# An allowance in the planner behind the comparisons of the later routing phases

## The chip, the cores and the metric

The kernel runs on one core of one Trainium2 chip. The metric is the device time of one execution in microseconds. A program is compiled once and run several times; the median of the runs is what counts.

## What is computed

Three layers follow one another: causal attention with decay (4 batches, 8 heads, 576 positions, head size 64), a dense layer with a squared ReLU (512 to 2048 to 512 on 2304 tokens), and a layer of eight experts (512 to 1024 to 512). The change is in the third. Every token goes to one expert, and each expert takes at most 288. The reference goes through all pairs of token and expert from the highest logit down:

```python
logits = x @ w_gate                       # 2304 x 8
order = np.argsort(-logits.flatten())
for idx in order:
    tok, e = int(idx) // E, int(idx) % E
    if assigned[tok] >= 0 or counts[e] >= cap:   # cap = 288
        continue
    assigned[tok] = e
    counts[e] += 1
...
for e in range(E):
    h = np.maximum(x[assigned == e] @ w1[e], 0.0)
    out[assigned == e] = h @ w2[e]
```

## The kernel before, in words

**Routing in phases.** The kernel does not sort. In each of eight phases (`phase(m)`, m from 0 to 7) it finds the expert that is the next to be full, the threshold at which that happens, and the tokens that it gets. Logits lie in a tile L of 128 partitions, 18 columns and 8 experts. A phase takes each token's best remaining expert (L1005 to L1018) and then finds the threshold in three rounds, digit by digit of the logit's bits (`RND`). In a round VectorE compares a digit with a row of numbers in three groups of six columns: OH (one-hot, L1053) and G (greater or equal, L1056). TensorE multiplies OH by G over 18 columns and so gets a histogram (L1067). VectorE copies two columns of it (h0, L390, a helper); TensorE sums over experts (L1072); VectorE forms rs, counts (L1074, L1078) and PB (L1081); TensorE sums again (T8, L1082), and the result gives the digit (th, L1083). After the third round come the small operations of the tail: ef, gx, mE, tie, ASG and the two masks M (L1105 to L1114), the expert's number ei (L1116), a prefix sum and a column sum by TensorE (L1122, L1124), and the positions (L1129 to L1145). A last comparison, OR (L1149, in the same buffer as OH), and TensorE's list matmul over 18 columns (L1163) put the token numbers in order; `lo` and `idx` (L1167, L1169) are copied from it. Phase 7 has no histogram: it gives what is left to the last expert, so it has only the tail and a list. Each phase needs the marks (ASG) and the remaining places (r, L1182) of the one before.

**Experts.** `expert(m)` gathers 288 rows through idx (three indirect DMAs of GpSimd, L1195), loads the weights of expert ei (SyncE reads the number from SBUF and issues eight loads, L1214 or L1228), transposes the rows (L1259), multiplies up (L1279) and down (L1308), transposes back (L1324) and scatters (L1331, GpSimd). Experts 0 to 4 multiply in plain float32. For experts 5 to 7 each weight is split into a rounded part (ScalarE, L386) and a remainder (GpSimd, 128x512 subtractions of L1234), and three products are added (L1283 to L1285, L1311 to L1313). Buffers that matter here: OH and G have one buffer each in all phases; idx has three, so idx of phase m waits until expert m - 3 has been scattered; raw weights have four.

**The order.** All work is given to a planner, `Sched`, as operations with the engines that can do them, a fixed duration for each, and the buffers read and written. It runs a list schedule of its own in planned time: an engine that is free takes, among the operations that are ready, the one with the smallest priority number. Phase m has 20 + m, expert m has 30 + m (28.5 + m for its gather), so a phase's operation goes ahead of any expert's as soon as it is ready. The order that comes out is written into the program engine by engine, and on the chip each engine keeps it: an engine that reaches an operation whose input is late stands still. When an operation ends in the plan, those that depend on it become ready after a latency by pair of engines, to which the operation can add an allowance of its own, `lag`:

```python
rt = now + LAT.get(t.eng, {}).get(e, 100.0) + t.lag
```

The allowance is in planned time only; nothing waits for it on the chip. The kernel before uses it in the weights of the dense layer and nowhere in the phases.

Of the kernel before, what the change touches and what calls it, by code (L numbers as in the profile page):

```python
# [14 lines left out]
OP = mybir.AluOpType  # L15
# [312 lines left out]
def dve2(n):  # L328
    return 70 + 0.52 * n
# [42 lines left out]
class K:  # L372
# [589 lines left out]
    def phase(self, m):  # L962
        s, lc, pp = self.s, self.lc, self.pp
        L, ASG, w8, i0, i1 = self.L, lc["ASG"], lc["w8"], lc["i0"], lc["i1"]
        last = m == E - 1
        ra, rows = 1 << RA, 8 << RA

        def T(shape, dt, tag, n=1):
            return s.buf(pp, shape, dt, "ph_" + tag, n)

        def v(fn, r, w, n=18, ap=0):
            s.op({"dve": 63.0 + 1.04 * n + (60 if ap else 0)}, fn, r=r, w=w)

        def small(tag="sm"):

            if m == 0 and tag in ("H", "pl"):
                return s.buf(self.ps, [128, 512], F, tag + "0", 0, also=[("pt", 0)] if tag == "H" else [("sc", 0), ("sc", 1)])
            return s.buf(self.ps, None, F, tag, 0, also=[("rt", 0)] if tag == "H" else [("rt", 1 + j) for j in range(NSM)])

        def pairs(a, n):  # L980
            return a.rearrange("p (b t) -> p b t", t=2)[:, :, None, :].to_broadcast([128, a.shape[1] // 2, n, 2])

        mE = T([128, 1], F, "mE")
        M = T([128, 2, 18], BF, "M")
        if last:
            v(lambda e: e.tensor_copy(mE.t, lc["SE"].t), [lc["SE"]], [mE], 1)
            fr = T([128, 18], F, "fr") if m else None
            v(lambda e: e.tensor_scalar(fr.t, ASG.t, 0.0, None, op0=OP.is_equal), [ASG], [fr])
            v(lambda e: e.scalar_tensor_tensor(M[:, 0, :], ASG.t, mE[:, 0:1], fr.t, op0=OP.is_equal, op1=OP.add), [ASG, fr, mE], [(M, 0)], ap=1)
            v(lambda e: e.tensor_copy(M[:, 1, :], lc["zz"][:, 0:18]), [lc["zz"]], [(M, 1)])  # L990
        else:
# [30 lines left out]
            for rd, (ba, bb_) in enumerate(RND):  # L1022
# [4 lines left out]
                q = T([128, 18], BF, "q")  # L1027
                bb = T([128, 18], BF, "bb")
# [17 lines left out]
                OH = T([128, 9, 128, 2], BF, "OH")  # L1046
                G = T([128, 9, 128, 2], BF, "G")
                hist = small("H")
                groups = [(0, 6, 0), (6, 12, 0), (12, 18, 1)] if m == 0 and rd == 0 else [(0, 6, None), (6, 12, None), (12, 18, None)]
                for g, (t0, t1, pi) in enumerate(groups):  # L1050
                    sl = slice(t0 // 2, t1 // 2)
                    nt = t1 - t0
                    s.op({"dve": dve2(nt * rows)}, lambda e, sl=sl, OH=OH, q=q, t0=t0, t1=t1, nt=nt: e.tensor_tensor(  # L1053
                        OH[:, sl, :rows], i1.t[:, None, :rows].to_broadcast([128, nt // 2, rows, 2]), pairs(q[:, t0:t1], rows), op=OP.is_equal),
                        r=[i1, (q, pi)], w=[(OH, g)])
                    s.op({"dve": dve2(nt * W)}, lambda e, sl=sl, G=G, bb=bb, W=W, t0=t0, t1=t1, nt=nt: e.tensor_tensor(  # L1056
                        G[:, sl, :W], pairs(bb[:, t0:t1], W), i0.t[:, None, :W].to_broadcast([128, nt // 2, W, 2]), op=OP.is_ge),
                        r=[i0, (bb, pi)], w=[(G, g)])

                    if m:  # L1060
                        if t1 < 18:
                            continue
                        t0 = 0

                    def hm(e, OH=OH, G=G, hist=hist, W=W, t0=t0, t1=t1):
                        for t in range(t0, t1):
                            e.matmul(hist[:rows, :W], OH[:, t // 2, :rows, t % 2], G[:, t // 2, :W, t % 2], start=(t == 0), stop=(t == 17))  # L1067
                    s.op({"pe": (t1 - t0) * HM}, hm, r=[(OH, g), (G, g)] if m == 0 else [OH, G], w=[hist])
# [75 lines left out]
        rb = T([128, 18], BF, "rb")  # L1144
        v(lambda e: e.scalar_tensor_tensor(rb.t, gm[:, :, 1], -96.0, rr.t, op0=OP.mult, op1=OP.add), [rr, (gm, 1)], [rb])  # L1145
        OR = T([128, 9, 128, 2], BF, "OH")
        for g in range(2):
            t0, t1 = (0, 8) if g == 0 else (8, 18)
            s.op({"dve": dve2(96 * (t1 - t0))}, lambda e, t0=t0, t1=t1: e.tensor_tensor(  # L1149
                OR[:, t0 // 2:t1 // 2, :96], i1.t[:, None, :96].to_broadcast([128, (t1 - t0) // 2, 96, 2]), pairs(rb[:, t0:t1], 96), op=OP.is_equal), r=[i1, rb], w=[(OR, g)])  # L1150
            if g == 0:
                gi = T([128, 18, 3, 2], BF, "gi")
                v(lambda e: e.tensor_tensor(gi.t, gm.t[:, :, :, None].to_broadcast([128, 18, 3, 2]), lc["ids"].t[:, :, None, :].to_broadcast([128, 18, 3, 2]), op=OP.mult), [gm, lc["ids"]], [gi], 108)
                pl = small("pl" if m == 0 else "sm")

            if m:
                if g == 0:
                    continue
                t0 = 0

            def lm(e, t0=t0, t1=t1):
                for t in range(t0, t1):
                    e.matmul(pl[:96, 0:6], OR[:, t // 2, :96, t % 2], gi[:, t].rearrange("p g d -> p (g d)"), start=(t == 0), stop=(t == 17))  # L1163
            s.op({"pe": (t1 - t0) * LM}, lm, r=[(OR, g) if m == 0 else OR, gi], w=[pl])
# [278 lines left out]
```

## Time and profile before

| | |
|---|---|
| median of 3 runs | 970.78 us (966.82 to 972.22) |
| the profiled execution | 967.55 us |
| its span, first to last instruction | 965.8 us |
| mean granted TensorE clock | 0.982 of full |
| TensorE busy | 913.3 us, 95% |
| VectorE, ScalarE, GpSimd busy | 658.8, 393.4, 352.2 us |

The profile is of one execution. A timeline row gives the start in us from the span's start, the length in us, the engine (PE is TensorE, DVE is VectorE, ACT is ScalarE, POOL is GpSimd, SPq the queue of DMAs that SyncE issues), the line, the operation, the tiles out<-in and the count of instructions merged into the row. What stands in brackets is the idle time of that engine before it and the work that ended it. The output of a matmul is named by its PSUM bank: `ov` is the bank of the phases. A float32 matmul has two records.

### The profile page before, as it was taken

How to read it: one execution, taken by the hardware profiler on the slowest of the kernel's cores; microseconds unless marked ns; L12 is line 12 of the kernel's file. 1: busy time of each engine (PE TensorE's matmuls, PEld its weight loads, DVE VectorE, ACT ScalarE, POOL GpSimd, SP SyncE). 2: the span in 40 equal slices, each digit the busy share in tenths (PEclk: the TensorE clock that was granted, in tenths of full speed). 3: DMA queues.
4: the chain of work that ended last, by engine and by line, in shares of the span. 5: the costliest groups of instructions: out<-in, count | busy, mean ns of one | idle time of the engine just before them, and what ended most of it. 6: DMA issues, size and time to landing. Idle time of an engine off the chain costs nothing. (4 is left out here: it accounts for less than half of the span.)

```text
span 965.8 us, 17449 instructions
## 1 busy us (share of the span) xinstructions
PE 913.3 (95%) x6087; PEld 737.0 (76%) x6087; DVE 658.8 (68%) x2078; ACT 393.4 (41%) x1075; POOL 352.2 (36%) x467
## 2 busy tenths in 40 slices
PE   6999898999999999999999999995999999999995
PEld 3555564767778989898989899774777777789995
DVE  5999999987436999999954322676777787422231
ACT  4777576656654344444434366000001122235310
POOL 2455565555234353535231100002003032657911
PEclk9999899999999999999999999995999999999998
DMA  5769686553314010101000000038535451434400
GB/s 201 239 216 277 212 252 218 173 163 113 109 42 158 22 44 1 45 1 44 1 23 1 23 1 1 12 110 275 165 124 182 175 159 39 142 116 158 133 26 26
DMA packets 48617, 106.72 MB, mean 111 GB/s; under 512 B 10280, under 2 KB 18632, under 8 KB 48400
## 3 DMA queue, kind: packets, MB, share of 16 engines
q1 hardware_dynamic: 45456, 96.16, 30.3%
q0 software_dynamic: 3072, 9.44, 3.3%
q8 instruction: 48, 0.79, 0.3%
q14 instruction: 41, 0.34, 0.1%
HBM read 91.25 MB, written 14.33 MB: 109 GB/s over the span
## 5 line engine op out<-in xcount | busy, mean ns | idle before, releaser
L694 PE MATMUL u<-xh,z 128*128 128x256 f32 x512 | 148.9, 291 | 0.4 <-ACT r L699 0.3
L696 PE MATMUL u<-xl,z 128*128 128x256 f32 x512 | 144.8, 283 | 0.0
L695 PE MATMUL u<-xh,z 128*128 128x256 f32 x512 | 144.8, 283 | 0.0
L711 POOL TENSOR_TENSOR hl<-r,hh 128x256 fp32r<-128x256 f32 x96 | 88.7, 926 | 132.3 <-ACT hh L386 116.9
L699 ACT ACTIVATE r<-u 128x256 f32<-128x256 f32 x144 | 54.7, 380 | 155.5 <-PE u L696 125.4
L863 DVE CUSTOM_DVE_ANT_0 gjk<-wof,wgb 128x512 bf16<-128x512 f32 x128 | 109.0, 852 | 1.4
L694 PEld LDWEIGHTS u<-xh,z 128*128 128x128 f32 x512 | 97.2, 190 | 13.2 <-issue 3.4
L695 PEld LDWEIGHTS u<-xh,z 128*128 128x128 f32 x512 | 97.3, 190 | 7.7
L696 PEld LDWEIGHTS u<-xl,z 128*128 128x128 f32 x512 | 97.2, 190 | 0.0
L720 PE MATMUL acc<-z,hl 128*128 128x512 f32 x224 | 88.3, 394 | 2.9 <-POOL hl L711 2.6
L718 PE MATMUL acc<-z,hh 128*128 128x512 f32 x224 | 89.6, 400 | 0.5 <-ACT hh L386 0.5
L1308 PE MATMUL acc<-ehh,z 128*128 128x288 f32 x320 | 89.0, 413 | 0.0
L719 PE MATMUL acc<-z,hh 128*128 128x512 f32 x224 | 88.9, 397 | 0.0
L1279 PE MATMUL u<-exh,z 128*128 128x288 f32 x304 | 86.8, 423 | 0.0
L1234 POOL TENSOR_TENSOR z<-wr,z 128x512 fp32r<-128x512 f32 x48 | 59.8, 1280 | 43.6 <-ACT z L386 43.5
L526 ACT ACTIVATE p<-p,st 128x448 f32<-128x448 f32 (+4 forms) x110 | 61.1, 556 | 31.2 <-DVE st L519 28.8
L514 POOL TENSOR_TENSOR row<-maskb,row 128x128 f32<-128x128 bf16 (+1 forms) x90 | 44.3, 497 | 74.6 <-DVE st L519 57.6
L1308 PEld LDWEIGHTS acc<-ehh,z 128*128 128x128 f32 x320 | 56.9, 190 | 14.0 <-issue 0.7
L1279 PEld LDWEIGHTS u<-exh,z 128*128 128x128 f32 x304 | 55.8, 195 | 14.5 <-ACT exh L386 0.3
L1195 POOL DMA_INDIRECT xg<-x2d,ph_idx x24 | 25.3, 1055 | 100.3 <-DVE ph_fr L1011 52.3
L1331 POOL DMA_INDIRECT out_dram<-yo,ph_idx x24 | 24.3, 1011 | 100.3 <-DVE ph_P L1097 32.3
L700 ACT ACTIVATE r<-r 128x256 f32<-128x256 f32 x138 | 57.7, 418 | 4.2
(349 smaller groups left out, 2213.9 us busy)
## 6 DMA issues: line engine op xcount, KB each, us to landing
z<-in_w_dram SPq DMA_DIRECT2D x40, 512.0 KB, 8.3
wr<-in_w_dram SPq DMA_DIRECT2D x24, 512.0 KB, 3.6
z<-in_w_in_dram SPq DMA_DIRECT2D x16, 512.0 KB, 5.5
z<-in_w_out_dram SPq DMA_DIRECT2D x14, 512.0 KB, 4.2
row<-cumd SPq DMA_DIRECT2D x24, 288.0 KB, 4.0
xd<-xo SPq DMA_DIRECT2D x16, 288.0 KB, 3.0
wraw<-rd SPq DMA_DIRECT2D x32, 128.0 KB, 3.2
xa<-xd SPq DMA_DIRECT2D x8, 512.0 KB, 4.3
```

Of the source, the lines that this page charges most:

```text
L526: s.op({"act": act(w, extra=2)}, lambda e, x=x, si=si, i=i, n=n, w=w, p=p[x], st=st[x]: e.activation(p[:n, :w], p[:n, :w], AF.Exp, bias=st ...
L694: e.matmul(u[:, :256], wh[:, k % 2, fs], xh[k][1](), start=(k == 0), stop=False)
L695: e.matmul(u[:, :256], wl[:, k % 2, fs], xh[k][1](), start=False, stop=False)
L696: e.matmul(u[:, :256], wh[:, k % 2, fs], xl[k][1](), start=False, stop=(k == 3))
L711: s.op(lo_alts(256), lambda e: e.tensor_sub(hl(), r.t, hh().bitcast(F)), r=[r, kh], w=[kl])
L718: g = [lambda e: e.matmul(acc.t, hh()[:, ts], wh[:, f % 2], start=(f == 0), stop=False), lambda e: e.matmul(acc.t, hh()[:, ts], wl[:, f % ...
L719: lambda e: e.matmul(acc.t, hh()[:, ts], wl[:, f % 2], start=False, stop=False),
L720: lambda e: e.matmul(acc.t, hl()[:, ts], wh[:, f % 2], start=False, stop=(f == 15))]
L863: s.op({"dve": dve1(DM) + 85}, lambda e, f=f, x=x, wo=wo, jk=jk: e.tensor_tensor_reduce(out=jk.t, in0=wo.t, in1=wb[:, x, :], scale=1.0, sc ...
L1234: s.op(lo_alts(512, LOE(m, which, i, 0, c)), lambda e, cs=cs: e.tensor_sub(lo[:, cs], raw[:, cs], hi[:, cs].bitcast(F)), r=[(raw, key), (h ...
L1279: s.op({"pe": 1.69 * CAP}, lambda e, k=k: e.matmul(u[:, :CAP], whi[0][k][:, fs], xh[k].t, start=(k == 0), stop=(k == 3)), r=[(whi[0][k], c ...
L1308: e.matmul(acc[:, :CAP], wh[:, ds], hh.t, start=(f == 0), stop=(f == 7))
```

## The change

Three operations of a phase get an allowance of 1500 ns in the plan, for phases with m of 3 and more: both comparisons before a histogram and the comparison before the list. The instructions stay the same in kind and number; the planner computes the order of all engines anew with it.

```diff
@@ phase(m)
         ra, rows = 1 << RA, 8 << RA
 
+        late = 1500.0 if m >= 3 else 0.0
+
...
                     s.op({"dve": dve2(nt * rows)}, lambda e, sl=sl, OH=OH, q=q, t0=t0, t1=t1, nt=nt: e.tensor_tensor(
                         OH[:, sl, :rows], i1.t[:, None, :rows].to_broadcast([128, nt // 2, rows, 2]), pairs(q[:, t0:t1], rows), op=OP.is_equal),
-                        r=[i1, (q, pi)], w=[(OH, g)])
+                        r=[i1, (q, pi)], w=[(OH, g)], lag=late)
                     s.op({"dve": dve2(nt * W)}, lambda e, sl=sl, G=G, bb=bb, W=W, t0=t0, t1=t1, nt=nt: e.tensor_tensor(
                         G[:, sl, :W], pairs(bb[:, t0:t1], W), i0.t[:, None, :W].to_broadcast([128, nt // 2, W, 2]), op=OP.is_ge),
-                        r=[i0, (bb, pi)], w=[(G, g)])
+                        r=[i0, (bb, pi)], w=[(G, g)], lag=late)
...
             s.op({"dve": dve2(96 * (t1 - t0))}, lambda e, t0=t0, t1=t1: e.tensor_tensor(
-                OR[:, t0 // 2:t1 // 2, :96], i1.t[:, None, :96].to_broadcast([128, (t1 - t0) // 2, 96, 2]), pairs(rb[:, t0:t1], 96), op=OP.is_equal), r=[i1, rb], w=[(OR, g)])
+                OR[:, t0 // 2:t1 // 2, :96], i1.t[:, None, :96].to_broadcast([128, (t1 - t0) // 2, 96, 2]), pairs(rb[:, t0:t1], 96), op=OP.is_equal), r=[i1, rb], w=[(OR, g)], lag=late)
```

## Rows read from the trace of the kernel before

**Rows 1.** The page's busy times and shares of the engines.

```profile
PE 913.3 (95%) x6087; PEld 737.0 (76%) x6087; DVE 658.8 (68%) x2078; ACT 393.4 (41%) x1075; POOL 352.2 (36%) x467
```

**Rows 2.** Busy us by stretch: length, then PE, PEld, DVE, ACT, POOL; PEclk, DMA, GB/s.

```profile
750.00:780.00 30.00, 30.00 (x198) 23.85 (x197) 21.92 (x100) 4.48 (x11) 3.00 (x5) 1.00 0.46 160
780.00:810.00 30.00, 28.58 (x188) 22.40 (x187) 23.89 (x101) 3.76 (x8) 6.26 (x5) 1.00 0.36 109
810.00:840.00 30.00, 26.51 (x154) 20.29 (x153) 17.83 (x59) 10.35 (x21) 19.02 (x20) 1.00 0.35 110
840.00:870.00 30.00, 30.00 (x140) 24.09 (x139) 7.72 (x19) 8.20 (x19) 18.07 (x20) 1.00 0.40 132
```

**Rows 3.** TensorE's timeline: start, length, line; idle before in brackets, with its releaser.

```profile
742.09 0.17 PE L1082 MATMUL ov<-ph_PB,rc_ones 128*128 128x8 bf16 x1 [0.38 <-DVE ph_idx L1169]
...
781.55 0.18 PE L1122 MATMUL ov<-ph_M,rc_pre 128*128 128x36 bf16 x1 [0.29 <-DVE ph_M L1114]
...
790.57 0.52 PE L1067 MATMUL ov<-ph_G,ph_OH 128*128 128x128 bf16 x6 [0.19 <-DVE ph_OH L1053]
...
791.57 0.50 PE L1067 MATMUL ov<-ph_G,ph_OH 128*128 128x128 bf16 x6 [0.47 <-DVE ph_G L1056]
...
792.50 0.50 PE L1067 MATMUL ov<-ph_G,ph_OH 128*128 128x128 bf16 x6 [0.43 <-DVE ph_G L1056]
...
819.32 1.19 PE L1163 MATMUL ov<-ph_gi,ph_OH 128*96 128x6 bf16 x18 [1.90 <-DVE ph_OH L1149]
...
826.51 1.20 PE L1163 MATMUL ov<-ph_gi,ph_OH 128*96 128x6 bf16 x18 [1.52 <-DVE ph_OH L1149]
...
904.17 0.30 PE L1259 MATMUL pt<-ident,xg 96*128 96x96 f32 x1 [1.68 <-DMA xg<-x2d,ph_idx]
```

**Rows 4.** TensorE's timeline, instructions without a gap before them.

```profile
755.35 0.96 PE L1163 MATMUL ov<-ph_gi,ph_OH 128*96 128x6 bf16 x18
...
799.75 1.19 PE L1067 MATMUL ov<-ph_G,ph_OH 128*128 128x128 bf16 x18
...
812.58 0.18 PE L1122 MATMUL ov<-ph_M,rc_pre 128*128 128x36 bf16 x1
...
858.25 0.51 PE L1283 MATMUL u<-exh,z 128*128 128x288 f32 x1
```

**Rows 5.** VectorE's timeline, phases 4 to 7.

```profile
780.55 0.15 DVE L1116 TENSOR_SCALAR ph_ei<-ph_mE 128x1 int32<-128x1 f32 x1
...
781.05 0.16 DVE L1169 SCALAR_TENSOR_TENSOR ph_idx<-ov,ph_lo 96x3 int32<-96x3 f32 x1 [0.35 <-issue]
...
786.23 2.69 DVE L1018 TENSOR_SCALAR ph_base<-ph_mx 128x18 f32<-128x18 f32 x1
...
798.67 0.55 DVE L1056 TENSOR_TENSOR ph_G<-ph_bb,rc_i 128x768 bf16<-128x768 bf16 x1
...
812.09 0.23 DVE L1114 TENSOR_SCALAR ph_M<-rc_ASG,ph_mE 128x18 bf16<-128x18 f32 x1
...
821.72 2.88 DVE L1132 SCALAR_TENSOR_TENSOR ph_M<-ph_scn,ph_M 128x18 bf16<-128x18 f32 x1
```

**Rows 6.** VectorE's groups by line and form, 690 to 780 us: busy, mean ns.

```profile
L1132 DVE SCALAR_TENSOR_TENSOR ph_M<-ph_scn,ph_M 128x18 bf16<-128x18 f32 x3 | 0.5, 171 | 0.0
```

**Rows 7.** GpSimd's timeline, its subtractions on the split weights.

```profile
786.39 2.49 POOL L1234 TENSOR_TENSOR z<-wr,z 128x512 fp32r<-128x512 f32 x2
...
813.49 3.74 POOL L1234 TENSOR_TENSOR z<-wr,z 128x512 fp32r<-128x512 f32 x3 [24.61 <-ACT z L386]
...
820.83 3.73 POOL L1234 TENSOR_TENSOR z<-wr,z 128x512 fp32r<-128x512 f32 x3
...
834.23 9.87 POOL L1234 TENSOR_TENSOR z<-wr,z 128x512 fp32r<-128x512 f32 x8 [2.63 <-ACT z L386]
```

**Rows 8.** The timeline of SyncE's DMA queue from 780 us.

```profile
781.48 7.76 SPq L1228 DMA_DIRECT2D wr<-in_w_dram  x5
```

**Rows 9.** ScalarE's timeline, the rounding of the split weights.

```profile
812.78 1.15 ACT L386 ACTIVATE z<-wr 128x512 fp32r<-128x512 f32 x2 [7.23 <-PE ov L1124]
```

## The prediction

> **What bounds the kernel now.** I read the page's busy shares first, then busy time by stretch, then TensorE's timeline with its idle gaps, and then what VectorE and GpSimd did in each gap. TensorE is busy 95% of the span [rows 1], so only time in which it stands still can be won. The change touches phases 3 to 6 (three histograms and a list each) and the list of phase 7, which ends at 826.51 + 1.20 = 827.71 us [rows 3]. Up to there TensorE is full from 750 to 780, and lacks 1.42 us between 780 and 810 and 3.49 us between 810 and 840; afterwards it is full again to 870 [rows 2]. A microsecond won or lost here therefore moves the end by a microsecond: no later gap absorbs it.
>
> The gaps themselves are few [rows 3]. Before the first histogram of phase 6 TensorE waits 0.19 + 0.47 + 0.43 = 1.09 us for OH and G; before the list of phase 6 it waits 1.90 us and before that of phase 7 1.52 us, both for OH of L1149. These sum to 4.51 us and are what a reserve behind OH and G can reach. Two more, 0.38 us (T8 matmul of L1082, behind an index) and 0.29 us (prefix matmul of L1122, behind M), stand at places that get no reserve. In a calm round VectorE is only just in time: the last G of a histogram ends at 798.67 + 0.55 = 799.22 and the matmul starts at 799.75; M ends at 812.09 + 0.23 = 812.32 and its matmul starts at 812.58 [rows 4, 5]. So the static order leaves about 0.5 us ahead of a histogram and 0.26 us ahead of the prefix matmul, and whatever makes VectorE later than that is a TensorE wait.
>
> What makes it late is the same each time. A small operation that takes 171 ns in calm stretches [rows 6] took 2.88 us at 821.72, and one at 786.23 took 2.69 us [rows 5]. Each ends within 0.05 us of the end of a run of GpSimd subtractions: 786.39 to 788.88, and 820.83 to 824.56 [rows 7]. The order was planned without this, since the planner has fixed durations per engine.
>
> **The change, part by part.** No instruction is added or removed. In the planner the matmul behind OH, G or OR counts as ready 1.5 us later, so some three expert matmuls (the planner's own cost for one is 1.69 x 288 = 487 ns) are put ahead of it.
>
> *What it wins.* With 1.5 us more in hand, at the same lateness, the three gaps become 0, 0.40 and 0.02 us: 4.09 of the 4.51 us. Upper bound 4.51, lower bound 0 (the wait comes back at another place).
>
> *What moves.* Each phase gets longer. Its three histograms are in series, and OH has one buffer, so the next phase's OH also waits for the list: up to 4 x 1.5 = 6 us a phase. The tail of phase 6 (L1105 to L1132) has passed four phases' worth of histograms and three lists, 12 x 1.5 + 3 x 1.5 = 22.5 us: its M goes from 812 to about 834, and the last list from 826 to about 850. TensorE's total work stays, since expert matmuls fill the room; of those there are enough, as it is full until 870 [rows 2].
>
> *The queues.* SP loads an expert's weights when the phase has written ei: L1116 at 780.55, first load of expert 5 at 781.48 [rows 5, 8], and behind that wait stand its seven other loads and those of later experts. Four such phases are moved; for expert 5 the shift is 16.5 us, to about 798. The cover: ScalarE's rounding of these weights stands still until 812.78, for slots that TensorE has to free [rows 9], and TensorE does not multiply by them before 858.25 [rows 4]. I price it at nothing; if the first cover were gone, the run of GpSimd behind it would start up to 16.5 us later, still 30 us ahead of that product. On the GpSimd queue the gathers wait for idx, and idx of phase 4 is written at 781.05 [rows 5] though its list ran at 755.35 [rows 4], 25 us earlier: it is not the phase that is late (three idx buffers). The shift of that list, 12 us, fits in. Priced at nothing; if the cover failed, the gather would delay its expert by what exceeds 25 us.
>
> *What it gives back.* This the trace does not show, as the moved tail meets other GpSimd runs. There are runs of 2, 3, 3 and then 8 subtractions, 9.87 us from 834.23 [rows 7]. In the kernel before the phases are over by then; moved by 22 us, the tail of phase 6 lies in that long run. Its operations lead to the prefix matmul, which has 0.26 us of cover and no reserve. From below: 0, if the run and the tail miss each other, or a small further gain where a run now meets no phase at all. From above: the run less the 2 us before the tail gets there, less the cover, 7.6 us. Between them I take the nearest row, one wait of VectorE for a GpSimd run with nothing behind it: 2.9 us [rows 5].
>
> By the Trainium skill (SBUF — State Buffer, Who interferes with whom) VectorE with two SBUF inputs and a GpSimd instruction exclude each other for one whole instruction, whichever was first. The trace agrees that they block; it differs in that the 2.88 us wait outlasted two boundaries between GpSimd instructions. By that rule the price would be one subtraction, 1.25 us, and the sum 968.0 us.
>
> *The sum.* -4.1 + 2.9 = -1.2 us. The profiled execution took 967.55 us (span 965.8 us), 3.2 us under the median of the three runs, 970.78 us; it becomes 966.4 us, and the median 969.6 us.
>
> **The rivals.**
> 1. *The tail falls into the long GpSimd run (slower).* Place: the prefix matmul L1122 of phase 6. Its operations between T8 and M are about eight, several with two SBUF inputs; if each waits for one subtraction of 1.25 us, the run is used up. Price 7.6 us, and two waits before T8 matmuls (also without reserve) in the runs of three, 0.85 us each (3.73 us is 40% of the 9.2 us from one histogram to the next, [rows 3, 4], and such a hit costs about 2 us): -4.1 + 7.6 + 1.7 = +5.2, 976.0 us. It decides from a give-back of 4.1 + 4.85 = 8.9 us on. For it: the shift of 22 us aims at 834. Against it: GpSimd's run starts when TensorE frees slots, and TensorE would be some microseconds ahead. Upper end, with the prefix matmul of phase 7 hit too: 978.
> 2. *All reachable gaps go, nothing comes back.* -4.5 us, 966.3 us. For it: between the runs of 3 and 8 there are free stretches of 3.6 and 9.7 us [rows 7]. Against it: 1.5 us does not cover 1.90.
> 3. *The spread order also removes the other waits (faster).* Add 0.38 and 0.29 us [rows 3], and 1.68 us before the last expert's transposes at 904.17 [rows 3], which hang on a gather: -4.5 - 2.35 = -6.9 us, 963.9 us. For it: the phases lie spread over a longer time, so VectorE's bursts collide less with gathers and copies. Against it: the last gather hangs on a scatter, not on phases.
> 4. *The reserve does nothing.* If the planner had put the same expert matmuls ahead anyway, 0 us, 970.8 us. Against it: the calm rounds show only 0.5 us.
>
> **How the numbers follow.** Half a percent, about what a measurement here can tell from none, is 4.85 us: 965.9 to 975.6. My forecast (0.32) and rivals 2 (0.13) and 4 (0.05) lie within: 0.50. Rival 3 has 0.24 and stands for every way in which the reshuffled order gains more than the named gaps; rival 1 has 0.26. The range reaches from below rival 3, 962.5, to the upper end of rival 1, 978. The forecast's own range, from no give-back to 4.5 us of it, is 966.3 to 971.2.
>
> **What would show it.** Right: no gap before L1067 and L1163 of phases 3 to 7 over 0.5 us; the list of phase 6 near 840, that of phase 7 near 850; first load of expert 5 near 798; a new gap of about 3 us, at L1122 or L1082, while a GpSimd run is going. For rival 1: several such gaps, between 830 and 845, with VectorE operations of over 1 us in a row. For rivals 2 and 3: TensorE full from 750 to 870. The prediction is wrong if TensorE lacks over 5 us between 780 and 870, if gathers or ScalarE's rounding become the releaser, or if the lists do not move.

## The result, and the profile after

The changed kernel is slower: 973.62 us median of 20 runs (968.95 to 979.9) against 968.45 us (964.57 to 974.7, 20 runs) of the kernel before on the same chip; ratio 1.0053, 95% interval 1.0035 to 1.007. That is +5.2 us where 1.2 us less was forecast. The profiled execution of the changed kernel took 974.59 us (span 972.8 us, 7.0 us more than before). Lines of the changed kernel stand 2 lower in the file from L968 on: L1067 is now L1069, L1122 is L1124, L1163 is L1165, L1234 is L1236.

First the page's busy times, where [rows 1] has 913.3 us for TensorE:

```profile
PE 916.5 (94%) x6087; PEld 739.2 (76%) x6087; DVE 666.4 (69%) x2081; ACT 391.9 (40%) x1072; POOL 353.2 (36%) x467
```

Busy time by stretch of the changed kernel; the columns are those of [rows 2].

```profile
780.00:810.00 30.00, 30.00 (x197) 23.88 (x196) 22.26 (x99) 4.45 (x10) 5.32 (x5) 1.00 0.35 115
810.00:840.00 30.00, 20.79 (x122) 15.70 (x121) 26.19 (x59) 8.73 (x20) 21.20 (x21) 0.92 0.32 99
840.00:870.00 30.00, 30.00 (x164) 24.13 (x162) 11.42 (x40) 8.47 (x19) 12.90 (x14) 0.97 0.33 105
...
830.00:835.00 5.00, 1.15 (x7) 0.68 (x6) 5.00 (x2) 2.34 (x5) 5.00 (x5) 1.00 0.13 39
835.00:840.00 5.00, 2.26 (x7) 1.54 (x7) 4.86 (x24) 0.00 (x0) 2.00 (x2) 0.51 0.15 36
840.00:845.00 5.00, 5.00 (x23) 4.10 (x22) 3.50 (x12) 1.45 (x3) 3.20 (x2) 0.81 0.76 232
```

From 780 to 810 TensorE is full now, where it lacked 1.42 us. From 810 to 840 it lacks 9.21 us instead of 3.49. The granted clock, 1.00 throughout in [rows 2], is 0.51 and 0.81 in the ten microseconds from 835, the end of the longest wait and what follows it: close to the lower of its two levels, 1.2 GHz, and then part of the time at 2.4.

TensorE's timeline of the changed kernel in this stretch, gaps in brackets:

```profile
825.45 0.52 PE L1069 MATMUL ov<-ph_G,ph_OH 128*128 128x64 bf16 x12 [2.41 <-DVE ph_idx L1171]
826.18 0.34 PE L1069 MATMUL ov<-ph_G,ph_OH 128*128 128x64 bf16 x6 [0.21 <-DVE ph_G L1058]
...
837.74 0.19 PE L1124 MATMUL ov<-ph_M,rc_pre 128*128 128x36 bf16 x1 [6.59 <-DVE ph_M L1116]
...
845.45 0.96 PE L1165 MATMUL ov<-ph_gi,ph_OH 128*96 128x6 bf16 x18
...
851.76 0.96 PE L1165 MATMUL ov<-ph_gi,ph_OH 128*96 128x6 bf16 x18
```

The waits before both lists, 1.90 and 1.52 us in [rows 3], are gone; two new ones, 2.41 and 6.59 us, have come. VectorE's timeline shows why:

```profile
817.94 5.37 DVE L1043 TENSOR_SCALAR ph_ti<-ph_P,ph_th 128x18 int32<-128x18 f32 x1
...
825.25 0.15 DVE L1171 SCALAR_TENSOR_TENSOR ph_idx<-ov,ph_lo 96x3 int32<-96x3 f32 x1
...
829.81 0.23 DVE L1107 SCALAR_TENSOR_TENSOR ph_ef<-ov,ph_th,rc_w 128x8 f32<-128x8 f32 x1
829.95 7.08 DVE L1110 SCALAR_TENSOR_TENSOR ph_gx<-ph_tu,ph_th,ph_mx 128x18 f32<-128x18 f32 x1
836.96 0.15 DVE L1111 TENSOR_REDUCE ph_mE<-ph_ef 128x1 f32<-128x8 f32 x1
837.03 0.22 DVE L1113 TENSOR_SCALAR ph_tie<-ph_tu,ph_th 128x18 f32<-128x18 f32 x1
```

and GpSimd's timeline what stood in its way:

```profile
817.38 0.92 POOL L1333 DMA_INDIRECT out_dram<-yo,ph_idx  x1 [0.20 <-issue]
818.32 4.94 POOL L1236 TENSOR_TENSOR z<-wr,z 128x512 fp32r<-128x512 f32 x4
...
828.68 0.92 POOL L1197 DMA_INDIRECT xg<-x2d,ph_idx  x1 [0.30 <-issue]
829.63 7.37 POOL L1236 TENSOR_TENSOR z<-wr,z 128x512 fp32r<-128x512 f32 x6
```

The operation of phase 6's tail that is held by the run of six (L1110) ends 0.03 us after it; the operations behind it are short again. The digit of round 3 (L1043) ends 0.05 us after the run of four. These two operations are the two new waits: M, which releases the prefix matmul, stands behind L1110, and idx (L1171), which releases the histogram, is among the operations that VectorE did without a pause behind L1043. Not every operation is held. The one just before L1110 (L1107) ran inside the run in 0.23 us; one of its inputs is in PSUM (`ov`), while L1110 and L1043 read SBUF alone.

**The balance.** TensorE's gaps of 0.15 us and more between 690 and 962 us sum to 7.18 us before and 12.42 us after: +5.24 us (+5.55 with the changed kernel's last wait, 0.31 us, which has moved out of the stretch to 962.76). An estimate of the lowered clock from the windows, busy time times what the clock lacks: 2.26 x 0.49 + 5.00 x 0.19 = 2.06 us. Together 7.3 to 7.6 us, where the spans of the two profiled executions differ by 7.0. The difference arises in this stretch: the list of phase 2 starts at 694.93 us before and 694.81 after, and from there to the end of the last matmul it is 7.1 us longer.

### The profile page after: what moved, and what is told of

The parts are those of the page before. It is cut to its first block, busy times and chain, and to the rows that moved or that the text cites. A ratio compares the mean times of both kernels' runs of the same rounds, so it can differ in the third digit from the quotient of the medians.

```text
span 972.8 us, 17451 instructions
## 1 busy us (share of the span) xinstructions
PE 916.5 (94%) x6087; PEld 739.2 (76%) x6087; DVE 666.4 (69%) x2081; ACT 391.9 (40%) x1072; POOL 353.2 (36%) x467
## 5 line engine op out<-in xcount | busy, mean ns | idle before, releaser
L711 POOL TENSOR_TENSOR hl<-r,hh 128x256 fp32r<-128x256 f32 x96 | 91.2, 952 | 130.9 <-ACT hh L386 110.7
L1236 POOL TENSOR_TENSOR z<-wr,z 128x512 fp32r<-128x512 f32 x48 | 61.1, 1306 | 48.5 <-ACT z L386 48.4
```

The costliest lines, as they stand in the source:

```text
L711: s.op(lo_alts(256), lambda e: e.tensor_sub(hl(), r.t, hh().bitcast(F)), r=[r, kh], w=[kl])
L1236: s.op(lo_alts(512, LOE(m, which, i, 0, c)), lambda e, cs=cs: e.tensor_sub(lo[:, cs], raw[:, cs], hi[:, cs].bitcast(F)), r=[(raw, key), (h ...
```

## The experiments

Three theories. **Collision:** the time is lost where a VectorE operation of a phase meets a GpSimd run. **Length:** phases that end later cost by themselves, in proportion. The third is on the size of a collision: what decides whether VectorE waits for one subtraction or for the whole run. Ratios are against the kernel before on the same chip (967.2 to 968.4 us), 12 runs each unless noted, with 95% intervals. "Gaps" is the sum over the same stretch as above (before: 7.18 us). Where an edit changes the planner's input (all but 3 and 6), the order of all engines is planned anew with it.

**1. The parts of the allowance.** Lists alone (e1), histograms alone (e2), phases 6 and 7 alone (e3):

```diff
# e1
-                        r=[i1, (q, pi)], w=[(OH, g)], lag=late)
+                        r=[i1, (q, pi)], w=[(OH, g)])
...
-                        r=[i0, (bb, pi)], w=[(G, g)], lag=late)
+                        r=[i0, (bb, pi)], w=[(G, g)])
# e2, at the end of the line of OR
-r=[i1, rb], w=[(OR, g)], lag=late)
+r=[i1, rb], w=[(OR, g)])
# e3
-        late = 1500.0 if m >= 3 else 0.0
+        late = 1500.0 if m >= 6 else 0.0
```

> Only the comparison before the list keeps the 1.5 us allowance (phases 3 to 7), the histograms lose it. Theory (a VectorE operation that meets a back-to-back run of GpSimd subtractions waits to the end of the run, so the cost depends on where the tails of the phases fall): the tail of phase 6 moves by 3 x 1.5 = 4.5 us, from 812 to about 816, among the runs of two to four subtractions; the waits of 1.90 and 1.52 us before the lists go, one wait of up to 3.7 us may come before the prefix matmul: -2 to +2 us against the kernel before. Rival (a longer chain costs by its length alone): 5 of the 17 allowances, a third of the +5.2 us of the whole change, +1.5 us.

> Only the histograms keep the allowance (phases 3 to 6), the lists lose it. Theory: the tail of phase 6 moves by 18 us, to about 828 to 830, where the long run of GpSimd subtractions starts; a wait of 4 to 7 us before the prefix matmul of phase 6, and the list waits come back where a run meets them: +2 to +7 us against before. Rival (length alone): 12 of 17 allowances, +3.7 us, spread over small waits and not in one.

> The allowance from phase 6 on only: three histograms and the lists of phases 6 and 7, where the kernel before has its 4.5 us of waits. The tail of phase 6 moves by 4.5 us only. Theory: the waits of 1.09, 1.90 and 1.52 us shrink to under 0.5 us each unless the tail now meets a run of three (up to 3.7 us): -4 to +1 us against before. Rival (length alone): 5 of 17 allowances, +1.5 us.

Measured: e1 0.9968 (0.9939 to 0.9996), gaps 5.83 us; e2 1.0038 (1.0016 to 1.006), gaps 11.94 us; e3 1.0006 (0.9981 to 1.0032), gaps 7.59 us. The part for the lists gains 3 us, a little more than the 2 us expected at best; the part for the histograms loses 3.7. In e2 the ys copy behind a 5.56 us operation (L1046) is 4.76 us late for TensorE, and M is 3.30 us late. In e1 the tail of phase 6 meets a GpSimd run too, but that costs only 2.43 us. VectorE's timeline of e1 there:

```profile
809.09 1.14 DVE L1110 SCALAR_TENSOR_TENSOR ph_gx<-ph_tu,ph_th,ph_mx 128x18 f32<-128x18 f32 x1
810.16 0.15 DVE L1111 TENSOR_REDUCE ph_mE<-ph_ef 128x1 f32<-128x8 f32 x1
810.23 1.23 DVE L1113 TENSOR_SCALAR ph_tie<-ph_tu,ph_th 128x18 f32<-128x18 f32 x1
...
811.53 1.17 DVE L1115 SCALAR_TENSOR_TENSOR ph_M<-ph_mx,ph_mE,ph_tie 128x18 bf16<-128x18 f32 x1
```

and the run, in GpSimd's timeline of e1:

```profile
808.93 3.73 POOL L1236 TENSOR_TENSOR z<-wr,z 128x512 fp32r<-128x512 f32 x3 [20.86 <-ACT z L386]
```

Here VectorE gets one turn after each subtraction, three in 3.73 us. In the changed kernel the same operation (L1110) got none in 7.37 us.

**2. Expert 5's remainders on VectorE**, so that no run of GpSimd subtractions is there to meet; in the changed kernel (e4) and in the kernel before (f4, 8 runs):

```diff
-LOE = lambda m,w,i,j,c: "dve pool" if m==0 else "pool"
+LOE = lambda m,w,i,j,c: "dve pool" if m==0 else "dve" if m==5 else "pool"
```

> The whole change, and the 16 subtractions for the split weights of expert 5 are planned on VectorE (about 0.6 us each) in place of GpSimd, so GpSimd has no run while the phases last. Theory: no small VectorE operation takes over 2 us between 790 and 855, the waits of 2.4 and 6.6 us in phase 6 go, and the time falls by 5 to 9 us against the changed kernel, to 0 to 4 us under the kernel before. Rival (length alone): the waits in phase 6 stay and the time is that of the changed kernel or longer by VectorE's extra 10 us of work.

> The kernel before with the 16 subtractions of expert 5 planned on VectorE, as in the run of the whole change with them there (which came out 1.7 us under before). Theory: the three waits of 1.1, 1.9 and 1.5 us go, -2 to -5 us against before; then the allowance in itself, without GpSimd runs, is worth about nothing (difference of the two runs under 3 us). Rival (length of the chain costs by itself): this run is 5 us or more faster than the other one.

Measured: e4 0.9983 (0.9954 to 1.0012), f4 0.9933 (0.9904 to 0.9961). Without the runs the changed kernel is about 7 us faster (1.0053 to 0.9983) and the one before about 6.5, more than the 5 expected at most. No VectorE operation of e4's phases takes over 0.9 us. But 4.8 us between e4 and f4 remain, where under 3 were expected, and e4 has one long gap that f4 has not, 4.10 us:

```profile
819.98 0.17 PE L1084 MATMUL ov<-ph_PB,rc_ones 128*128 128x8 bf16 x1 [4.10 <-DVE ph_idx L1171]
```

In VectorE's timeline of e4 its releaser waits for a scatter:

```profile
819.77 0.16 DVE L1171 SCALAR_TENSOR_TENSOR ph_idx<-ov,ph_lo 96x3 int32<-96x3 f32 x1 [4.57 <-DMA out_dram<-yo,ph_idx]
```

The list of phase 5 holds its PSUM slot until idx is copied, idx has only three buffers, and the T8 matmul (L1084) needs the slot. The scatter was late in its turn. GpSimd's and VectorE's timelines of e4:

```profile
809.01 4.59 POOL L1333 DMA_INDIRECT out_dram<-yo,ph_idx  x1 [26.72 <-DVE ph_OH L1055]
...
815.16 0.92 POOL L1333 DMA_INDIRECT out_dram<-yo,ph_idx  x1 [0.21 <-issue]
...
810.31 2.49 DVE L1236 TENSOR_TENSOR z<-wr,z 128x512 fp32r<-128x512 f32 x4
```

The first of its three issues took 4.59 us, where the third took 0.92, and ended 0.81 us after VectorE's subtractions (812.80). That this 3.7 us passed on to the wait of 4.10 is read from the trace, not tested; experiment 4 meets the same collision again.

**3. A pause without idleness.** A memset on GpSimd ahead of each subtraction, order unchanged: in the changed kernel (f1), the kernel before (f2) and the lists alone (f3).

```diff
# in the middle of the line of the subtraction
-lambda e, cs=cs: e.tensor_sub(lo[:, cs], raw[:, cs], hi[:, cs].bitcast(F))
+lambda e, cs=cs: (e.memset(self.spacer.t, 0.0), e.tensor_sub(lo[:, cs], raw[:, cs], hi[:, cs].bitcast(F)))
```

> The whole change, its static order untouched; GpSimd writes a one-element memset (about 0.1 us) before each of its 48 subtractions. Theory (VectorE waits to the end of a back-to-back run because no subtraction lets it in between): the break lets VectorE in after each subtraction, no small operation takes over 1.5 us, the wait of 2.4 us before the third histogram of phase 6 goes, that of 6.6 us before the prefix matmul falls to 2.4 to 5 us (several operations that wait once each): 2 to 6 us faster than the changed kernel. Rival (the run is held whatever stands in it): waits of 5 and 7 us stay, 0 to +1 us.

> The kernel before with the same memset before each of the 48 subtractions, order untouched. Theory: the operations of 2.69 and 2.88 us fall to 1.5 us or less each, the wait before the list of phase 7 (1.52 us) shrinks to about zero, that before the list of phase 6 (a run in which VectorE already got its turns) stays near 1.9 us: 1 to 3 us faster than before. Rival: same waits, 0 to +1 us.

> Allowance on the lists only, with the memset before each subtraction. In the lists-only run VectorE got a turn after each subtraction anyway, so theory: no more than 1 us either way against lists only, that is -2 to -4 us against before. Rival: the same, so this run is for the best version, not for telling them apart.

Measured: f1 1.0029 (1.0005 to 1.0052), f2 0.9991 (0.9966 to 1.0016), f3 0.9971 (0.9945 to 0.9997). f1 is 2.3 us under the changed kernel, with overlapping intervals; f2, of which 1 to 3 us were expected, is no different from the kernel before. And VectorE's two long operations in f1, from which 1.5 us at most was expected, are still 5.45 and 5.94 us. GpSimd and VectorE in f1's timelines:

```profile
831.44 0.09 POOL L1236 MEMSET spacer<- 1x1 f32 x1
831.49 1.25 POOL L1236 TENSOR_TENSOR z<-wr,z 128x512 fp32r<-128x512 f32 x1
...
829.35 5.94 DVE L1110 SCALAR_TENSOR_TENSOR ph_gx<-ph_tu,ph_th,ph_mx 128x18 f32<-128x18 f32 x1
```

An instruction of GpSimd between two subtractions does not let VectorE in: that idea fell.

**4. Eight index buffers instead of three,** alone in both kernels (g1 after, g2 before) and with the remainders on VectorE (g3 after, g4 before). g2 and g4 have 6 runs, g3 has 10.

```diff
-        idx = T([96, 3], I32, "idx", 3)
+        idx = T([96, 3], I32, "idx", 8)
```

> The whole change with eight idx buffers in place of three, so that an index is written right behind its list and no longer waits for the scatter of the expert three before. GpSimd's subtractions stay on GpSimd. Theory (the loss of the whole change is VectorE held by GpSimd's runs in phase 6): the wait of 5 to 7 us before the prefix matmul of phase 6 stays, the time is 0 to 3 us under the changed kernel, still 2 to 5 us over before. Rival (index waits are the loss): about the time of before or less.

> The kernel before with eight idx buffers. Its only index wait in the routing is 0.4 us and the last expert's gather costs 1.7 us: -2 to +0.5 us against before by the theory; by the rival, the same.

> The whole change with the 16 subtractions of expert 5 on VectorE and eight idx buffers. In the run without the buffers the T8 matmul of phase 6 stood 4.1 us behind the index of phase 5. Theory: that wait goes, no gap over 1 us is left in the phases, 3 to 5 us under that run, 5 to 8 us under before, and within 2 us of the same two edits on the kernel before. Rival (a longer chain costs by its length alone): 5 us over the same two edits on the kernel before, as without the buffers.

> The kernel before with the 16 subtractions of expert 5 on VectorE and eight idx buffers. Without the buffers it came out 6.5 us under before. Theory and rival: no gap over 1 us in the phases, 6 to 9 us under before; it is the partner of the run of the whole change with the same two edits.

Measured: g1 1.0044 (1.0022 to 1.0066), g2 0.9935 (0.9916 to 0.9955), g3 0.9968 (0.9949 to 0.9988), g4 0.9907 (0.9885 to 0.993). The kernel before gains by both edits, by the buffers alone 6.3 us, where nothing to 2 us was expected; g4, 958.44 us, is the fastest of all. g1 keeps its loss: its longest wait, 5.67 us before a T8 matmul, stands behind an operation held for 6.22 us (L1083). The changed kernel with both edits is still some 6 us behind g4, where 2 at most were expected, with one gap of 7.33 us. TensorE, GpSimd and VectorE in g3's timelines:

```profile
821.71 0.39 PE L1261 MATMUL pt<-ident,xg 96*128 96x96 f32 x1 [7.33 <-DMA xg<-x2d,ph_idx]
...
809.94 6.06 POOL L1197 DMA_INDIRECT xg<-x2d,ph_idx  x1 [28.68 <-PE pt L1261]
816.30 0.92 POOL L1197 DMA_INDIRECT xg<-x2d,ph_idx  x1 [0.30 <-issue]
...
809.90 0.55 DVE L1055 TENSOR_TENSOR ph_OH<-rc_i,ph_q 128x768 bf16<-128x768 bf16 x1
...
812.71 2.49 DVE L1236 TENSOR_TENSOR z<-wr,z 128x512 fp32r<-128x512 f32 x4
```

It is the collision the other way round: the issue of a gather takes 6.06 us instead of 0.92, and ends 0.80 us after VectorE's unbroken burst (815.20).

**5. Length or place.** 500 ns (h1), 3000 ns (h2), 1500 ns in phases 3 to 5 alone (h3); and the lists' allowance with both edits of 2 and 4 (h4).

```diff
 h1: late = 500.0 if m >= 3 else 0.0
 h2: late = 3000.0 if m >= 3 else 0.0
 h3: late = 1500.0 if m in (3, 4, 5) else 0.0
```

> The allowance is 500 ns instead of 1500 ns, on the same three operations of phases 3 and later. Theory length (a later end of the phases costs by itself): a third of the shift, so a third of +5.2 us: about +1.7 us, 1.0018. Theory collision (the cost is where the small operations of a phase meet GpSimd's subtractions or gather issues): not in proportion; the time differs from the kernel before by about the difference of the waits of over 0.15 us between 690 and 960 us, each with a VectorE operation of over 2 us or a GpSimd issue of over 3 us as its cause, and may have either sign.

> The allowance is 3000 ns instead of 1500 ns. Theory length: twice the shift, about +10 us, 1.011, whatever the waits. Theory collision: not in proportion. The tail of phase 6 would be moved by up to 45 us, to about 857, behind the long run of GpSimd that it met at 829.6 with 1500 ns; if it lands in a gap between runs, the time is nearer to before than with 1500 ns (+0 to +4 us), and a wait of over 5 us at the prefix matmul is not there.

> The allowance of 1500 ns stands in phases 3, 4 and 5 alone; phases 6 and 7 have none. Theory length: phase 6 still begins some 16 us later than in the kernel before, so most of the loss stays, +3.5 us. Theory collision: the tail of phase 6 comes some 4.5 us earlier than in the changed kernel, near 825 to 833, so it still meets the run at 818 to 823 or that from 829.6; a wait of over 2 us at the prefix matmul or at the list of phase 6 goes with a VectorE operation that ends with the run; +2 to +6 us if so, and within 2 us of before if neither is met.

> Three parts together: the allowance on the lists alone, expert 5's remainders on VectorE instead of GpSimd, and eight index buffers instead of three. The parts alone or in pairs gave -3 us (lists), -6.5 us (remainders on VectorE without the allowance), -9 us (remainders and eight buffers without the allowance). If the gain of the lists stands by itself: -10 to -12 us, 0.988, and the best of all. If it was the same waits that the other two parts remove (which collision theory says, since without GpSimd's run there is nothing for OR to be late for): -9 us, 0.991, no better than without the allowance; if the 7 us of shift bring a gather issue into a burst of VectorE, as in the changed kernel with both parts, -3 us.

Measured: h1 0.9979 (0.9951 to 1.0007), gaps 5.73 us; h2 1.0101 (1.0071 to 1.013), gaps 16.38 us; h3 1.001 (0.9982 to 1.0038), gaps 8.55 us; h4 0.9942 (0.9913 to 0.997), gaps 4.12 us. Length asked for 1.0018 at 500 ns, which lies outside h1's interval, and for 1.011 at 3000 ns, which lies inside h2's. My collision theory missed h2: I expected at most +4 us and no long wait. VectorE and GpSimd in h2's timelines:

```profile
812.17 7.69 DVE L1019 TENSOR_TENSOR ph_sg<-ph_sg,ph_kf 128x18 uint32<-128x18 uint32 x1
...
812.44 7.38 POOL L1236 TENSOR_TENSOR z<-wr,z 128x512 fp32r<-128x512 f32 x6
```

The tail of phase 6 is out of the way, but the start of the phase stands in a run of six instead. So the time follows the waits, not the length: over the two kernels and all 18 experiments (the two below with them), the sum of the gaps and the time have a correlation of 0.93, at 1.2 us of time for 1 us of gap. The place of the last list correlates with the time too (0.83), but the six kernels that have it between 846 and 852 us differ from 0.9968 (g3) to 1.0053 (the changed kernel). What length does, on this reading, is to give the phases more GpSimd runs and gathers to meet. h4's single gap of 3.44 us stands behind a copy of ScalarE that waits for a scatter, one of whose issues took 2.99 us; the lists' allowance, worth 3 us by itself, costs 3.4 once the two edits are there (g4 to h4).

**6. What decides one turn or none.** In the 18 profiles up to here (the kernels before and after and e1 to h4) 15 small VectorE operations, of up to 18 columns, took over 2 us; each ends within 0.1 us of the end of a GpSimd run, and every one of these runs stands right behind an indirect DMA issue of GpSimd (in f1 and f2 with the memset between). Some of the 15 began while the issue still ran (L1043 at 817.94), some in the middle of the run (5.37 us from 832.56, in h2's run from 830.53). Two large comparisons were held by such runs too, for 4.08 us in h3 and 4.73 in f3. In the runs that begin from a wait for ScalarE, 41 operations of up to 144 columns took 1.0 to 1.4 us and none more. So the last two runs put a moment of idleness between issue and run, in the changed kernel (h5) and in the one before (h6), when the order is written out (`sub` marks the subtractions):

```diff
...
+ if t.eng == "pool":
+     if self.was_dma and getattr(t, "sub", False):
+         pg = self.pools["spacer"].tile([1, 2], F, name="pingpong", tag="pingpong", bufs=1)
+         nc.gpsimd.memset(pg[:, 0:1], 0.0)
+         nc.scalar.activation(pg[:, 1:2], pg[:, 0:1], AF.Copy)
+         nc.gpsimd.memset(pg[:, 1:2], 0.0)
+     self.was_dma = t.nbytes > 0
...
```

> The order of the changed kernel is kept. In front of a run of GpSimd's subtractions that stands right behind an indirect DMA issue, three tiny instructions are put in: a memset on GpSimd, a copy of it by ScalarE, and a memset on GpSimd that waits for this copy, so that GpSimd stands idle for a moment before the run. Theory idle (what a run holds is kept from the DMA issue on until GpSimd first stands idle): VectorE gets its turn after each subtraction, no VectorE operation takes over 1.4 us, the tail of phase 6 in the run of six has four such turns, so its wait falls from 6.6 us to some 4 us; 3 to 4 us less than the changed kernel, ratio about 1.001 to 1.003. Theory lead (a run holds because its inputs are all there, however it begins): VectorE's operations still take the whole run, 5.4 and 7.1 us, and the ratio stays about 1.005. In both, a GpSimd idle of more than 1 us before the run, behind a busy ScalarE, would show as a longer wait of the product by these weights instead.

> The same three instructions in the kernel before, whose order is kept. Theory idle: the two VectorE operations of 2.69 and 2.88 us become 1.2 us and less; the later of them leads to the last list, whose wait of 1.52 us shrinks or stays as several operations each wait 1.2 us: -1 to 0 us. Theory lead: both operations stay above 2.4 us, and the time stays within 1 us of before.

Measured: h5 1.0008 (0.9986 to 1.0029), h6 1.0003 (0.9978 to 1.0027). Lines here stand 8 lower than in the changed kernel. GpSimd, VectorE and TensorE in h5's timelines:

```profile
824.95 0.92 POOL L1205 DMA_INDIRECT xg<-x2d,ph_idx  x1 [0.30 <-issue]
825.86 0.09 POOL L319 MEMSET pingpong<- 1x1 f32 x1
826.38 0.09 POOL L321 MEMSET pingpong<- 1x1 f32 x1 [0.42 <-issue]
826.43 7.42 POOL L1244 TENSOR_TENSOR z<-wr,z 128x512 fp32r<-128x512 f32 x6
...
828.36 0.60 DVE L1118 SCALAR_TENSOR_TENSOR ph_gx<-ph_tu,ph_th,ph_mx 128x18 f32<-128x18 f32 x1
...
828.95 1.24 DVE L1121 TENSOR_SCALAR ph_tie<-ph_tu,ph_th 128x18 f32<-128x18 f32 x1
...
830.25 1.18 DVE L1123 SCALAR_TENSOR_TENSOR ph_M<-ph_mx,ph_mE,ph_tie 128x18 bf16<-128x18 f32 x1
831.36 1.30 DVE L1124 TENSOR_SCALAR ph_M<-rc_ASG,ph_mE 128x18 bf16<-128x18 f32 x1
...
832.71 0.18 PE L1132 MATMUL ov<-ph_M,rc_pre 128*128 128x36 bf16 x1 [3.16 <-DVE ph_M L1124]
```

The run is as long as before (six in 7.42 us), the tail still stands in it, and now it gets a turn after each subtraction: no small operation of h5 takes over 1.4 us, and the wait of 6.59 us is 3.16 (some 4 was expected). The idle time is 0.29 and 0.42 us. The gaps sum to 8.20 us instead of 12.42. This took 4.4 us of the 5.2 off the changed kernel. In h6 the operations of 2.69 and 2.88 us are gone as well (1.56 us at most), but several operations wait one after the other and the list of phase 6 still waits 1.86 us: no gain, where 0 to 1 us was expected.

## Why the prediction was wrong, step by step

- **What bounds the kernel** held: the time follows TensorE's gaps in this stretch.
- **What it wins.** 4.09 of 4.51 us were forecast, and all 4.51 were won: the lists' 3.42 us and the 1.09 us before the first histogram of phase 6 are gone. But 2.41 + 0.21 = 2.62 us stand before the third histogram of that phase now, since a reserve of 1.5 us does not cover an operation of 5.37 us.
- **What moves** was about right: the list of phase 6 is at 845.45 (forecast 840), that of phase 7 at 851.76 (850), the first load of expert 5 at 793.77 (798). Without its wait the tail would have formed M near 831 (834).
- **The queues** were rightly priced at nothing: in the changed kernel no weight load and no rounding releases TensorE late. That idx waits for a scatter was seen, but not that the list's PSUM slot waits with it; this showed in e4 (the 0.38 us behind an index in [rows 3] is its small form).
- **What it gives back is the step that failed.** I bounded it from 0 to 7.6 us and took the nearest row, 2.9 us. It is 6.59 us at the prefix matmul and 2.62 before the histogram, 9.2 in all, above the 8.9 us from which my first rival was to decide. That rival had the place and nearly the price (7.6 + 1.7 = 9.3 us, +5.2 us in all, against +5.2 measured); that its sum agrees to the tenth is luck, since 7.6 stands for 6.59, 1.7 for 2.62 at another matmul, and the clock is not in it. I held against it that TensorE, some microseconds ahead, would free slots sooner and start GpSimd's run earlier. The run did start earlier, at 829.63 instead of 834.23 (whether for this reason no run shows), and the tail came at 829.95, straight into it. The row of 2.9 us was a wait for the rest of a run of three; what I should have scaled was the length of the run that stands at the new place.
- **How the rival worked** was not as I put it. Not eight operations used up the run with one subtraction each: one operation waited for all of it. The 2.88 us row had shown this already, as the prediction says, and the price of one boundary (1.25 us) fell with it. The run that I read the danger from, eight from 834.23, begins from a wait for ScalarE [rows 7]; such runs gave VectorE a turn after each subtraction wherever they met it (experiment 6). The new order put the run of six right behind the gather's issues, and that made it hold.
- **The clock** was left out: a mean of 0.66 in the ten microseconds from 835, some 2 us.
- **A slip in the sums.** The forecast's own range, from no give-back on, begins at 966.3 us, which is the second rival's figure; with 4.09 us won it would be 966.7.

## What to carry to other kernels

A reserve in a static order moves everything behind it, and the price is what the moved work meets at its new place, not the gap that it had: read there, for each engine that shares something with it, the longest unbroken run. Two edits that took the collision away (work on another engine, more index buffers) gained 9 us here, and the reserve on top of them only lost. Where GpSimd issues an indirect DMA and then computes, a short wait for another engine between the two is worth trying when VectorE has urgent small work: it took 4.4 us off one order here (h5) and nothing off the other (h6).

## What the runs showed of the hardware

- **GpSimd can keep VectorE out over many instructions.** Right behind an indirect DMA issue, a run of two to eight subtractions (1.23 us each) blocked a small VectorE operation to its end, up to 7.69 us; 0.29 to 0.42 us of idleness between issue and run turned this into one turn after each subtraction. A memset of 0.09 us, before the run and between its subtractions, did not (f1). Whether it is the idleness itself or the wait for another engine's signal, these runs do not tell apart.
- By the Trainium skill (SBUF — State Buffer, Who interferes with whom) whoever is first has the shared port for the whole of one instruction. The runs that begin from a wait agree (1.0 to 1.4 us); the ones behind a DMA issue do not (5.37 and 7.08 us), and there the measurement decides.
- **The other way round,** VectorE's unbroken operations with two SBUF inputs held an indirect DMA issue for 6.06 us instead of 0.92 (g3), and in the kernel before one of 2.85 us at 735.86 ended 0.8 us after a burst of comparisons. In the 20 profiles 11 such issues took 2.85 us or more, and each ended 0.80 to 0.82 us after the burst.
- The Trainium skill (SBUF — State Buffer, Who interferes with whom) infers that VectorE's tensor_tensor leaves descriptor generation alone; g3's issue, held while VectorE did nothing but tensor_tensor, does not agree.
- **TensorE's clock fell around its longest wait:** the granted clock is 0.51 and 0.81 in the ten microseconds from 835, and the wait of 6.59 us ends at 837.74; the kernel before, with no wait over 1.90 us there, stays at 1.00 from 780 to 870 [rows 2].
